# Padded, full-array attention products for the 64 last rows of each sequence, placed behind w_in's, in a two-layer kernel

## The chip, the cores and the metric

The kernel runs on one core of a Trainium2 chip. The metric is the device time of one execution in microseconds, the median of several runs. A profiled execution has a span (first to last instruction) and a time of its own.

## What is computed

Attention with a sliding window of 128 keys and a linear bias per head, then two feed-forward layers over the 2304 rows (4 sequences of 576), all in fp32. Cut to what matters, the reference is:

```python
batch, n_heads, seq, head_dim = (4, 8, 576, 64)
scores = scale * q @ k.T                       # per batch and head
scores = where((rel >= 0) & (rel < 128), scores + slopes[h] * -abs(rel), -1e9)
attn = softmax(scores)                         # over the keys
x = (attn @ v).transpose(0, 2, 1, 3).reshape(B * S, H * D)       # 2304 x 512
h = x @ w_in;  x = relu(h) ** 2 @ w_out        # 512 -> 2048 -> 512
h = x @ w2_in; x = (h * tanh(softplus(h))) @ w2_out
```

## The kernel before

The 2304 rows are cut into five **blocks** (`blocks`, lines 118 to 124): block 0 is rows 0 to 511 of sequence 0, block 1 gathers the **last 64 rows** (512 to 575) of all four sequences, blocks 2 to 4 are rows 0 to 511 of sequences 1 to 3. All five pass through layer 1, then all five through layer 2, in the order 0, 2, 3, 4, 1; so block 1 is stored last.

Attention is cut into **units**: a unit of kind "q" is 256 query rows of one head, a unit of kind "e" the last 64 rows of one sequence for two heads, e = 0 and 1, that lie in the two halves of the partitions. Units 0 to 15 (block 0) run ahead of everything; units 16 to 31 are the 16 "e" units of block 1; units 32 to 79 are "q" units of blocks 2 to 4. The main loop (lines 694 to 740) runs block j through layer 1 in 16 **steps** `fc`, one per 128 columns of w_in, and beside each step of block j goes one unit of block j + 1, in three stages spread over three steps: scores and softmax of unit i + 2, transposition of unit i + 1, value products of unit i. So the "e" units run beside the steps of j = 0. The order on each engine is the order in which the program writes the instructions.

One step of the program, in order: `w_tick1` (j = 0 only: prepares weights on ScalarE, L109 and L85), `u_softmax2` (normalises p of unit i + 1), `front` (loads, and `u_scores` of unit i + 2), `relu2_b` (L577, VectorE: low part g[1] of the previous step), `u_softmax1`, `w_tick2` (VectorE: L91, L94, L97, L114, and the weights' load L80), `m_h` (12 products x by w_in into h: L483 to L485), `relu2_a` (ScalarE: r, then squares gg and g: L566, L569, L572), the first half of `m_out` (g by w_out of the previous step: L511 to L513), a second weights' tick, `turned` (`u_transpose` L376, copy L397, two GpSimd selections L399 that write pT), the second half of `m_out`. The value products `u_av` (L448 for "e" units, L434 for "q" units) stand behind `relu2_a`, but for "e" units from fc = 1 on (`soon`) right behind `front`, ahead of `m_h`.

Products of layer 1 and 2 are done in three parts of a one-pass 32-bit type (hi by hi, lo by hi, hi by lo). The "e" units and block 0's units use plain fp32 products. An "e" unit's scores (L311) are two products of 64 rows by 64 columns of the array, one per head in its own quadrant, 192 columns long; its values (L448) are four products whose results go to 64 of the array's 128 columns: two over 128 keys (urv) and two over 64 (urw), each 64 columns long. A "q" unit's values (L434) likewise go to one column half per head. PSUM tiles of scores, transposed p and values come from a ring of three (`ps_a`); h has one tile. pT of units from 16 on has one buffer.

Loads are all issued by SyncE (SP) in program order. An "e" unit loads q and k (L225, one load), v (L238) and the last 64 keys' v (L239, two buffers). At the end `m_evac` (lines 555 to 558) copies block 1's result (L540 on ScalarE, L541 on VectorE) and stores it with two loads-out of 256 KB from SP, each two sequences.

Of the kernel before, what the change touches and what calls it, by code (L numbers as in the profile page):

```python
# [8 lines left out]
F32 = mybir.dt.float32  # L9
# [5 lines left out]
ALU = mybir.AluOpType  # L15
# [3 lines left out]
P = 128  # L19
B, H, S, D = 4, 8, 576, 64  # L20
# [13 lines left out]
def two_layers(  # L34
# [16 lines left out]
    nc = tc.nc  # L51
# [76 lines left out]
    x32 = {}  # L128
# [78 lines left out]
    def u_load(i):  # L207
        kind, j, off, b, s0, h = units[i]
        u = ustate[i] = Unit()
        if i < NU0:  # L210
            return
        if place[i] not in raws:
            raws.clear()
            raws[place[i]] = ap["raw"].tile([P, 640], F32, tag="uraw", name=f"uraw{i}")
        u.raw = raws[place[i]]
        if kind == "q":
            u.nk = 384 if s0 else 256
            u.nb = u.nk // P
            r = rows(i)
            nc.sync.dma_start(  # L220
                out=u.raw[r, 0 : 256 + u.nk],
                in_=qkT[b, h, r, 2 * s0 : 2 * s0 + 256 + u.nk],
            )
        else:
            nc.sync.dma_start(out=u.raw[:, 0:256], in_=qkE[b, h])  # L225

    def u_vload(i):
        kind, j, off, b, s0, h = units[i]
        if i < NU0:
            return  # L230
        u = ustate[i]
        u.rv = ap["raw"].tile([P, 3, D], F32, tag="urv", name=f"urv{i}", bufs=4)
        if kind == "q":
            k0 = 1 if s0 else 0
            nc.sync.dma_start(out=u.rv[:, 0 : u.nb, :], in_=vP[b, h, :, k0 : k0 + u.nb, :])
        else:
            u.rw = ap["raw"].tile([64, 2, D], F32, tag="urw", name=f"urw{i}")
            nc.sync.dma_start(out=u.rv[:, 0:2, :], in_=vE[b, h])  # L238
            nc.sync.dma_start(out=u.rw, in_=vF[b, h])  # L239

    def u_split(i):
        kind, j, off, b, s0, h = units[i]
# [40 lines left out]
    def u_scores(i):  # L283
        kind, j, off, b, s0, h = units[i]
        u = ustate[i]
        u.ps = ps_a.tile([P, 2, 256], F32, tag="a", name=f"sc{i}")
        if kind == "q":
            for s in range(2):
                k0 = s * P if s0 else 0
                n = 256 if s0 or s else P  # L290
                o = u.ps[:, s, 256 - n :]
                if i < NU0:

                    q, kv = pair[h // 2]
                    c, m = 2 * s0 + h % 2 * 256 + s * P, max(0, s0 + s * P - P)
                    nc.tensor.matmul(o, q[:, c : c + P], kv[:, m : m + n], start=True, stop=True)
                    continue
                if plain_s(i):
                    qk = u.raw[rows(i)]
                    sq, kk = qk[:, s * P : (s + 1) * P], qk[:, 256 + k0 : 256 + k0 + n]  # L300
                    nc.tensor.matmul(o, sq, kk, start=True, stop=True)
                    continue
                sq = u.hi[:, s * P : (s + 1) * P]
                nc.tensor.matmul(o, sq, u.hi[:, 256 + k0 : 256 + k0 + n], start=True, stop=False)  # L304
                nc.tensor.matmul(o, sq, u.lo[:, k0 : k0 + n], start=False, stop=True)  # L305
        else:

            for e in range(2):
                own = slice(e * D, (e + 1) * D)
                o, qk = u.ps[own, 0, 0:192], u.raw[own]  # L310
                nc.tensor.matmul(o, qk[:, 0:D], qk[:, D:256], start=True, stop=True)  # L311

    def probs(i, s):
        kind, j, off, b, s0, h = units[i]
# [63 lines left out]
    def u_unfold(i):  # L378

        kind, j, off, b, s0, h = units[i]  # L380
        u = ustate[i]
        e = 0 if kind == "e" else i % 2
        if e:
            u.pT = ustate[i - 1].pT
        elif i < NU0:
            t = wp.tile([P, 2 * DM], F32, tag=f"wh{8 + i // 2 % 4}", name=f"pT{i}")
            u.pT = t.rearrange("p (e m c) -> p e m c", e=2, m=4)
        else:
            u.pT = ap["w"].tile([P, 2, 4, P], F32, tag="pT", name=f"pT{i}", bufs=1)
        if i < NU0:  # L390
            copy = nc.vector.tensor_copy if i == NU0 - 1 else nc.scalar.copy
            a = 0 if s0 else 1
            copy(u.pT[:, e, a:, :], u.pt[:, a:, :])
            return

        n, m = (2, P) if kind == "q" else (1, D)
        nc.scalar.copy(u.p[:, 0:n], u.pt[:, 0:n])  # L397
        for k, a, r, sign, op in ((0, 0 if s0 else 1, P, 1, ALU.is_gt), (1, 0, m, -1, ALU.is_ge)):
            nc.gpsimd.affine_select(  # L399
                out=u.pT[0:r, e, k : 2 * n : 2, :][:, a:],  # L400
                in_=u.p[0:r, a:n],
                pattern=[[0, n - a], [0, P // m], [-sign, m]],
                compare_op=op,
                fill=0.0,
                base=0,
                channel_multiplier=sign,
            )

    def u_av(i):
# [32 lines left out]
            ustate.pop(i - 1)  # L442
        else:
            o = ps_a.tile([P, 512], F32, tag="a", name=f"o{i}")
            for blk, (r, v) in enumerate(((P, u.rv), (64, u.rw))):
                for e in range(2):
                    c = slice(e * D, (e + 1) * D)
                    nc.tensor.matmul(  # L448
                        o[c, 0:D], v[:, e, :], u.pT[0:r, 0, blk, c], start=blk == 0, stop=blk == 1
                    )  # L450
            nc.scalar.copy(x32[j][h][:, off : off + D], o[:, 0:D])
        ustate.pop(i)


# [67 lines left out]
    def m_evac(l, j, parts=(0, 1)):  # L522
# [11 lines left out]
        for p in parts:  # L534
# [13 lines left out]
            if len(runs) == 1:  # L548
# [2 lines left out]
                dst = out[row : row + 2 * P, :].rearrange("(e p) d -> p e d", e=2)  # L551
                nc.sync.dma_start(out=dst, in_=ev)
                continue
            ends = out.rearrange("(b s) d -> b s d", b=B)
            for e in range(2):
                b = 2 * (2 * p + e)
                s0, m = runs[b][1:]
                nc.sync.dma_start(out=ends[b : b + 2, s0 : s0 + m, :], in_=ev[:, e, :])

    def relu2_a(j, fc):  # L560
        n = size[j]
# [24 lines left out]
    ap["raw"] = actx.enter_context(tc.tile_pool(name="araw", bufs=2))  # L586
    ap["spl"] = actx.enter_context(tc.tile_pool(name="aspl", bufs=2))
    ap["w"] = actx.enter_context(tc.tile_pool(name="aw", bufs=2))
    bias_sb = ap["w"].tile([P, 1 + H, 256], BF16, name="bias_sb", bufs=1)
    biasA_sb = wp.tile([P, 2 * DM], F32, tag="wh7", name="biasA_sb")  # L590
    biasA_sb = biasA_sb.bitcast(BF16).rearrange("p (h c) -> p h c", h=H)
# [29 lines left out]
    def turned(i):  # L621
        u_transpose(i)
        u_unfold(i)
# [70 lines left out]
    for j in range(NB - 1):  # L694
        for fc in range(FC):
            step = j * FC + fc
            last = fc == FC - 1
            av, tr, sc = ([i] if i < NU else [] for i in range(NU0 + step, NU0 + step + 3))
            soon = units[av[0]][0] == "e" and fc > 0
            if j == 0:  # L700
                w_tick1(0)
            for i in tr:
                u_softmax2(i)
            for i in sc:
                front(i)
            for i in av if soon else []:
                u_av(i)
            if pend is not None:
                relu2_b(pend)
            for i in sc:  # L710
# [5 lines left out]
                for c in range(2):  # L716
                    x_split(j + 1, c, xp)
            pend = relu2_a(j, fc)
            for i in av if not soon else []:
                u_av(i)  # L720
            if last:
                for c in range(2, KC):
                    x_split(j + 1, c, xp)
            if prev is not None:
                m_out(*prev, 0)
            if j == 0 and turn["at"] < NW + 4:
                w_tick(0)
            for i in tr:
                turned(i)
            if prev is not None:  # L730
                m_out(*prev, 1)
# [181 lines left out]
```

## Time and profile before

| | |
|---|---|
| runs | 943.62, 945.62, 945.96 us; median 945.62 |
| profiled execution: its time, its span | 945.08 us, 943.3 us |
| busy: TensorE, VectorE, ScalarE, GpSimd | 96%, 43%, 44%, 21% |
| w_in products of block 0 (16 steps), first and last start | 41.83 and 157.85 us |

The page shows for each engine the time in which it executed something, and the list of waits what ended the idle stretches. Products overlap: the start of one to the start of the next is what a product costs, not its duration. An order of instructions in time is read per engine; a number in brackets is the idle time just before the instruction, with the instruction that ended it. The view by stretches gives the length, then each engine's busy time and count (PE, PEld for weight loads, DVE, ACT, POOL), the clock granted to TensorE, the DMA engines' busy share and GB/s. PE is TensorE, DVE VectorE, ACT ScalarE, POOL GpSimd, SPq SyncE's queue.

### The profile page before, as it was taken

How to read it: one execution, taken by the hardware profiler on the slowest of the kernel's cores; microseconds unless marked ns; L12 is line 12 of the kernel's file. 1: busy time of each engine (PE TensorE's matmuls, PEld its weight loads, DVE VectorE, ACT ScalarE, POOL GpSimd, SP SyncE). 2: the span in 40 equal slices, each digit the busy share in tenths (PEclk: the TensorE clock that was granted, in tenths of full speed). 3: DMA queues.
4: the chain of work that ended last, by engine and by line, in shares of the span. 5: the costliest groups of instructions: out<-in, count | busy, mean ns of one | idle time of the engine just before them, and what ended most of it. 6: DMA issues, size and time to landing. Idle time of an engine off the chain costs nothing.

```text
span 943.3 us, 13014 instructions
## 1 busy us (share of the span) xinstructions
PE 909.6 (96%) x4680; PEld 743.1 (79%) x4680; DVE 409.1 (43%) x1043; ACT 419.5 (44%) x1017; POOL 200.1 (21%) x314
## 2 busy tenths in 40 slices
PE   7989999999999999999999999999999999999993
PEld 5666667999778877887788888888888888888893
DVE  6887887665433353333699662111212111111110
ACT  6866665666554455444577633222212222222220
POOL 4311114676555555552000000000000000000000
PEclk9999999999999999999999999999999999999997
DMA  8365551433222222230664430020002000200100
GB/s 238 125 201 167 166 173 60 138 87 91 80 61 53 62 92 65 78 102 1 202 199 157 134 112 1 1 89 1 1 1 90 1 0 1 67 1 1 45 1 23
DMA packets 40293, 74.71 MB, mean 79 GB/s; under 512 B 4388, under 2 KB 18340, under 8 KB 40228
## 3 DMA queue, kind: packets, MB, share of 16 engines
q1 hardware_dynamic: 40228, 73.88, 24.9%
q8 instruction: 37, 0.61, 0.3%
q14 instruction: 28, 0.23, 0.1%
HBM read 64.42 MB, written 9.44 MB: 78 GB/s over the span
## 4 chain that ended last, share of the span: by engine, by line
PE 87%; ACT 6%; DVE 2%; POOL 2%; issue 1%; SPq 1%; DMA 1%; POOLq 0%; DVEq 0%
PE h L483 14%; PE h L484 14%; PE h L485 14%; PE o L516 7%; PE o L517 7%; PE o L518 7%; PE o L511 6%; PE o L512 6%; PE o L513 6%; PE o L434 3%; POOL pT L399 1%; PE sc L305 1%; PE sc L304 1%; PE pt L376 1%; ACT gg L569 1%; ACT r L566 1%
## 5 line engine op out<-in xcount | busy, mean ns | idle before, releaser
L483 PE MATMUL h<-xh,wh 128*128 128x512 f32 (+1 forms) x640 | 238.5, 373 | 1.5 <-ACT r L566 1.5
L484 PE MATMUL h<-xl,wh 128*128 128x512 f32 (+1 forms) x640 | 236.4, 369 | 0.0
L485 PE MATMUL h<-xh,wl 128*128 128x512 f32 (+1 forms) x640 | 236.0, 369 | 0.0
L760 ACT ACTIVATE t<-h 128x512 f32<-128x512 f32 (+1 forms) x80 | 44.4, 555 | 290.3 <-PE h L485 215.9
L766 DVE TENSOR_TENSOR g<-t,g 128x512 fp32r<-128x512 f32 (+1 forms) x80 | 50.9, 636 | 203.8 <-ACT g L761 203.8
L483 PEld LDWEIGHTS h<-xh,wh 128*128 128x128 f32 x640 | 120.8, 189 | 22.7 <-ACT r L566 2.0
L485 PEld LDWEIGHTS h<-xh,wl 128*128 128x128 f32 x640 | 121.0, 189 | 20.7
L484 PEld LDWEIGHTS h<-xl,wh 128*128 128x128 f32 x640 | 121.1, 189 | 19.2
L511 PE MATMUL o<-g,wh 128*128 128x512 f32 (+1 forms) x320 | 126.0, 394 | 0.0
L512 PE MATMUL o<-g,wh 128*128 128x512 f32 (+1 forms) x320 | 118.5, 370 | 1.2 <-DVE g L577 1.2
L513 PE MATMUL o<-g,wl 128*128 128x512 f32 (+1 forms) x320 | 118.4, 370 | 0.0
L516 PE MATMUL o<-wh,g 128*128 128x512 f32 x288 | 112.2, 390 | 0.0
L517 PE MATMUL o<-wl,g 128*128 128x512 f32 x288 | 112.2, 390 | 0.0
L518 PE MATMUL o<-wh,g 128*128 128x512 f32 x288 | 112.0, 389 | 0.0
L339 ACT ACTIVATE p<-p,st 128x128 f32<-128x128 f32 (+1 forms) x144 | 59.5, 415 | 85.8 <-DVE st L328 85.7
L399 POOL TENSOR_SCALAR_AFFINE_SELECT pT<-p 128x256 f32<-128x256 f32 (+2 forms) x128 | 59.0, 480 | 131.1 <-ACT p L397 130.5
L577 DVE TENSOR_TENSOR g<-gg,g 128x512 fp32r<-128x512 f32 (+1 forms) x80 | 57.6, 720 | 55.8 <-POOL gg L571 53.6
L566 ACT ACTIVATE r<-h 128x512 f32<-128x512 f32 (+1 forms) x80 | 44.0, 549 | 84.4 <-PE h L485 84.4
L511 PEld LDWEIGHTS o<-g,wh 128*128 128x128 f32 x320 | 60.1, 188 | 13.4 <-issue 2.2
L512 PEld LDWEIGHTS o<-g,wh 128*128 128x128 f32 x320 | 60.4, 189 | 10.3 <-DVE g L577 2.3
L513 PEld LDWEIGHTS o<-g,wl 128*128 128x128 f32 x320 | 60.2, 188 | 10.5
L518 PEld LDWEIGHTS o<-wh,g 128*128 128x128 f32 x288 | 54.1, 188 | 11.5
(69 smaller groups left out, 1172.4 us busy)
## 6 DMA issues: line engine op xcount, KB each, us to landing
wraw<-in_w SPq DMA_DIRECT2D x64, 512.0 KB, 4.3
uraw<-in_qkT SPq DMA_DIRECT2D x24, 320.0 KB, 3.0
uraw<-in_qkT SPq DMA_DIRECT2D x24, 256.0 KB, 2.7
x<-x1d SPq DMA_DIRECT2D x16, 256.0 KB, 4.3
out_x<-ev SPq DMA_DIRECT2D x8, 512.0 KB, 2.9
x1d<-ev SPq DMA_DIRECT2D x10, 256.0 KB, 2.3
urv<-in_vP SPq DMA_DIRECT2D x24, 96.0 KB, 2.6
uraw<-in_qkE SPq DMA_DIRECT2D x16, 128.0 KB, 2.0
```

What stands on the lines that cost most here:

```text
L339: nc.scalar.activation(probs(i, s), probs(i, s), AF.Exp, bias=u.st[:, s : s + 1], scale=-1.0, accum_out=u.st[:, 2 + s : 3 + s],)
L399: nc.gpsimd.affine_select(out=u.pT[0:r, e, k : 2 * n : 2, :][:, a:], in_=u.p[0:r, a:n], pattern=[[0, n - a], [0, P // m], [-sign, m]], com ...
L483: nc.tensor.matmul(ph[:, 0:n], wh[:, cs], xh[:, 0:n], start=c == 0, stop=False)
L484: nc.tensor.matmul(ph[:, 0:n], wh[:, cs], xl[:, 0:n], start=False, stop=False)
L485: nc.tensor.matmul(ph[:, 0:n], wl[:, cs], xh[:, 0:n], start=False, stop=c == KC - 1)
L511: nc.tensor.matmul(o[:, r], wh[:, ws], g[:, 0, r], start=first, stop=False)
L512: nc.tensor.matmul(o[:, r], wh[:, ws], g[:, 1, r], start=False, stop=False)
L513: nc.tensor.matmul(o[:, r], wl[:, ws], g[:, 0, r], start=False, stop=last)
L516: nc.tensor.matmul(o, g[:, 0, es], wh[:, ws], start=first, stop=False)
L517: nc.tensor.matmul(o, g[:, 0, es], wl[:, ws], start=False, stop=False)
L518: nc.tensor.matmul(o, g[:, 1, es], wh[:, ws], start=False, stop=last)
L577: nc.vector.tensor_tensor(g[:, 1, 0:n], gg[:, 0:n], g[:, 0, 0:n].bitcast(F32), op=ALU.subtract)
```

## The change

The "e" units' products use the whole array. q of the two heads is loaded into the two diagonal quarters of a 128 x 128 tile `qd` (two buffers, zero elsewhere, set once by GpSimd), so one product of 192 columns gives both heads' scores. v of the last 64 keys is loaded into the upper half of `vd` (three buffers, lower half zero), and two products of 128 columns give the values of both heads, each with the other head's probabilities as well; two copies of 64 x 64 on ScalarE take the two diagonal quarters. The second GpSimd selection covers 128 rows instead of 64. `soon` is gone: the values of all units stand behind `relu2_a`. For j > 0 `turned` stands right behind the values, ahead of the first half of `m_out`. pT has two buffers. Block 1's last store is four stores of 128 KB, one per sequence, in turn from SP and ScalarE's queue.

```diff
@@ u_load
-            nc.sync.dma_start(out=u.raw[:, 0:256], in_=qkE[b, h])
+            u.qd = qd[i % len(qd)]
+            for e in range(2):
+                c = slice(e * D, (e + 1) * D)
+                nc.sync.dma_start(out=u.qd[c, c], in_=qkE[b, h, c, 0:D])
+            nc.sync.dma_start(out=u.raw[:, 0:192], in_=qkE[b, h, :, D:256])
@@ u_vload
-            u.rw = ap["raw"].tile([64, 2, D], F32, tag="urw", name=f"urw{i}")
+            u.rw = vd[i % len(vd)]
             nc.sync.dma_start(out=u.rv[:, 0:2, :], in_=vE[b, h])
-            nc.sync.dma_start(out=u.rw, in_=vF[b, h])
+            nc.sync.dma_start(out=u.rw[0:64], in_=vF[b, h])
@@ u_scores
-            for e in range(2):
-                own = slice(e * D, (e + 1) * D)
-                o, qk = u.ps[own, 0, 0:192], u.raw[own]
-                nc.tensor.matmul(o, qk[:, 0:D], qk[:, D:256], start=True, stop=True)
+            nc.tensor.matmul(
+                u.ps[:, 0, 0:192], u.qd, u.raw[:, 0:192], start=True, stop=True
+            )
@@ u_unfold
-            u.pT = ap["w"].tile([P, 2, 4, P], F32, tag="pT", name=f"pT{i}", bufs=1)
+            u.pT = ap["w"].tile([P, 2, 4, P], F32, tag="pT", name=f"pT{i}", bufs=2)
...
-        for k, a, r, sign, op in ((0, 0 if s0 else 1, P, 1, ALU.is_gt), (1, 0, m, -1, ALU.is_ge)):
+        for k, a, sign, op in ((0, 0 if s0 else 1, 1, ALU.is_gt), (1, 0, -1, ALU.is_ge)):
             nc.gpsimd.affine_select(
-                out=u.pT[0:r, e, k : 2 * n : 2, :][:, a:],
-                in_=u.p[0:r, a:n],
+                out=u.pT[:, e, k : 2 * n : 2, :][:, a:],
+                in_=u.p[:, a:n],
@@ u_av
-            for blk, (r, v) in enumerate(((P, u.rv), (64, u.rw))):
-                for e in range(2):
-                    c = slice(e * D, (e + 1) * D)
-                    nc.tensor.matmul(
-                        o[c, 0:D], v[:, e, :], u.pT[0:r, 0, blk, c], start=blk == 0, stop=blk == 1
-                    )
-            nc.scalar.copy(x32[j][h][:, off : off + D], o[:, 0:D])
+            for blk, v in enumerate((u.rv[:, 0:2, :], u.rw)):
+                v = v.rearrange("p e d -> p (e d)")
+                nc.tensor.matmul(
+                    o[:, 0:P], v, u.pT[:, 0, blk, :], start=blk == 0, stop=blk == 1
+                )
+            for e in range(2):
+                c = slice(e * D, (e + 1) * D)
+                nc.scalar.copy(x32[j][h][c, off : off + D], o[c, c])
@@ m_evac
-            ends = out.rearrange("(b s) d -> b s d", b=B)
-            for e in range(2):
-                b = 2 * (2 * p + e)
-                s0, m = runs[b][1:]
-                nc.sync.dma_start(out=ends[b : b + 2, s0 : s0 + m, :], in_=ev[:, e, :])
+            for k, (b, s0, m) in enumerate(runs):
+                row = b * S + s0
+                src = ev[k % 2 * m : (k % 2 + 1) * m, k // 2, :]
+                (nc.sync, nc.scalar)[k % 2].dma_start(out=out[row : row + m, :], in_=src)
@@ two_layers, ahead of the loads
+    qd = [ap["raw"].tile([P, P], F32, name=f"qd{n}", bufs=1) for n in range(2)]
+    vd = [ap["raw"].tile([P, 2, D], F32, name=f"vd{n}", bufs=1) for n in range(3)]
+    for t in qd + vd:
+        nc.gpsimd.memset(t, 0.0)
@@ main loop
-            soon = units[av[0]][0] == "e" and fc > 0
...
-            for i in av if soon else []:
-                u_av(i)
...
             pend = relu2_a(j, fc)
-            for i in av if not soon else []:
+            for i in av:
                 u_av(i)
+            for i in tr if j > 0 else []:
+                turned(i)
...
-            for i in tr:
+            for i in tr if j == 0 else []:
                 turned(i)
             if prev is not None:
                 m_out(*prev, 1)
```

Where this moves TensorE's instructions is seen in two places. The first is the step fc = 6 of j = 0, from the end of the step before (names: sc scores, o with pT values, h the w_in products, o_0 the w_out products, pt the transposition). Before:

```order
L513 MATMUL o_0_3_727<-g_0_4_965,wl_4_837 128x512
L311 MATMUL sc_1087<-uraw_928 64x192 x2
L448 MATMUL o_1096<-pT_1069,urv_930 64x64 x2
L448 MATMUL o_1096<-pT_1069,urw_931 64x64 x2
L483 MATMUL h_0_6_1114<-xh_309,wh_6_998 128x512
...
L485 MATMUL h_0_6_1114<-xh_588,wl_6_999 128x512
L511 MATMUL o_0_0_724<-g_0_5_1046,wh_5_917 128x512
```

With the change:

```order
L519 MATMUL o_0_3_739<-g_0_4_969,wl_4_848 128x512
L312 MATMUL sc_1095<-uraw_937,qd_99 128x192
L489 MATMUL h_0_6_1116<-xh_323,wh_6_1007 128x512
...
L491 MATMUL h_0_6_1116<-xh_602,wl_6_1008 128x512
L452 MATMUL o_1135<-pT_1077,urv_941 128x128
L452 MATMUL o_1135<-pT_1077,vd_102 128x128
L517 MATMUL o_0_0_736<-g_0_5_1049,wh_5_927 128x512
```

The values have moved from ahead of the twelve w_in products to behind them, and both groups have half as many, wider products.

The second place is a step of block 2 with values. Before, TensorE's order behind its w_in products is:

```order
L485 MATMUL h_2_5_3343<-xh_2953,wl_5_918 128x512
L434 MATMUL o_3362<-pT_3246,urv_3138 64x256
...
L434 MATMUL o_3362<-pT_3246,urv_3200 64x128
L511 MATMUL o_2_0_3100<-g_2_4_3294,wh_4_836 128x512
...
L513 MATMUL o_2_1_3101<-g_2_4_3294,wl_4_837 128x512
L376 MATMUL pt_3374<-ident,p_3274 128x128 x2
L511 MATMUL o_2_2_3102<-g_2_4_3294,wh_4_836 128x512
```

With the change:

```order
L491 MATMUL h_2_5_3337<-xh_2954,wl_5_928 128x512
L438 MATMUL o_3356<-pT_3234,urv_3132 64x256
...
L438 MATMUL o_3356<-pT_3234,urv_3194 64x128
L379 MATMUL pt_3362<-ident,p_3268 128x128 x2
L517 MATMUL o_2_0_3101<-g_2_4_3288,wh_4_847 128x512
...
L519 MATMUL o_2_1_3102<-g_2_4_3288,wl_4_848 128x512
L517 MATMUL o_2_2_3103<-g_2_4_3288,wh_4_847 128x512
```

The transpositions now follow the values directly, and the twelve w_out products are no longer parted.

## Rows read from the trace of the kernel before

**Rows 1.** The page: busy time of the engines; TensorE's granted clock by slices.

```profile
PE 909.6 (96%) x4680; PEld 743.1 (79%) x4680; DVE 409.1 (43%) x1043; ACT 419.5 (44%) x1017; POOL 200.1 (21%) x314
...
PEclk9999999999999999999999999999999999999997
```

**Rows 2.** List of waits: engine, line, releaser, us in total, times, longest.

```profile
PE o L448 <- POOL pT L399: 9.8, 27, 2.7
```

**Rows 3.** TensorE in order of time: start us, us, line, [idle before].

```profile
80.90 0.50 PE L483 MATMUL h<-xh,wh 128*128 128x512 f32 x1
...
86.73 0.54 PE L311 MATMUL sc<-uraw 64*64 64x192 f32 x4
87.46 0.34 PE L448 MATMUL o<-pT,urv 128*64 128x64 f32 x4 [0.19 <-POOL pT L399]
88.15 0.33 PE L448 MATMUL o<-pT,urw 64*64 64x64 f32 x4 [0.35 <-POOL pT L399]
88.42 0.50 PE L483 MATMUL h<-xh,wh 128*128 128x512 f32 x1
```

**Rows 4.** ScalarE in order of time, the same step.

```profile
83.98 0.60 ACT L566 ACTIVATE r<-h 128x512 f32<-128x512 f32 x1 [2.35 <-PE h L485]
...
86.74 0.24 ACT L397 COPY p<-pt 128x128 f32<-128x128 f32 x1
...
88.53 0.21 ACT L451 COPY x<-o 128x64 f32<-128x64 f32 x1 [0.15 <-PE o L448]
```

**Rows 5.** GpSimd in order of time, the same step.

```profile
87.12 0.98 POOL L399 TENSOR_SCALAR_AFFINE_SELECT pT<-p 128x128 f32<-128x128 f32 x2 [6.53 <-ACT p L397]
```

**Rows 6.** VectorE in order of time, the same step.

```profile
84.54 0.69 DVE L97 SCALAR_TENSOR_TENSOR wf<-wraw,wf 128x512 int32<-128x512 int32 x1
86.30 0.69 DVE L114 TENSOR_TENSOR wl<-wf,wh 128x512 fp32r<-128x512 f32 x1 [1.07 <-ACT wh L109]
```

**Rows 7.** TensorE in order of time, units of block 0.

```profile
31.61 0.60 PE L373 MATMUL pt<-ident,p 128*128 128x128 f32 x4
32.05 1.03 PE L296 MATMUL sc<-kv,qq 128*128 128x256 f32 x4
32.91 0.49 PE L373 MATMUL pt<-ident,p 128*128 128x128 f32 x3
```

**Rows 8.** TensorE in order of time, two steps of block 2.

```profile
273.90 0.39 PE L513 MATMUL o<-g,wl 128*128 128x512 f32 x1
...
274.58 0.40 PE L512 MATMUL o<-g,wh 128*128 128x512 f32 x1
...
278.72 0.39 PE L485 MATMUL h<-xh,wl 128*128 128x512 f32 x1
...
280.39 0.39 PE L512 MATMUL o<-g,wh 128*128 128x512 f32 x1
```

**Rows 9.** Busy time in one stretch; PEclk is the granted clock.

```profile
50.00:60.00 10.00, 9.46 (x44) 6.99 (x43) 7.62 (x19) 6.45 (x17) 0.98 (x2) 0.86 0.54 179
```

**Rows 10.** VectorE in order of time, steps 0 and 1 of block 0.

```profile
45.52 0.69 DVE L114 TENSOR_TENSOR wl<-wf,wh 128x512 fp32r<-128x512 f32 x1
...
51.86 0.69 DVE L114 TENSOR_TENSOR wl<-wf,wh 128x512 fp32r<-128x512 f32 x1
```

**Rows 11.** TensorE in order of time, w_in's first product of fc = 2.

```profile
58.42 0.50 PE L483 MATMUL h<-xh,wh 128*128 128x512 f32 x1
```

**Rows 12.** VectorE, ScalarE, TensorE in order of time, end of block 0.

```profile
142.15 1.11 DVE L97 SCALAR_TENSOR_TENSOR wf<-wraw,wf 128x512 int32<-128x512 int32 x1
...
151.47 0.60 ACT L566 ACTIVATE r<-h 128x512 f32<-128x512 f32 x1 [1.92 <-PE h L485]
...
164.61 0.50 PE L512 MATMUL o<-g,wh 128*128 128x512 f32 x1 [1.24 <-DVE g L577]
```

**Rows 13.** The page's DMA issues: count, KB each, us to landing.

```profile
x1d<-ev SPq DMA_DIRECT2D x10, 256.0 KB, 2.3
```

**Rows 14.** SP in order of time: the last two stores before.

```profile
929.12 1.33 SPq L558 DMA_DIRECT2D out_x<-ev  x2
```

## The prediction

> **What bounds the kernel now.** I read the page first. TensorE is busy in 96% of the span and its clock stands at the upper level nearly throughout [rows 1], so there is little idle time to win, and the list of waits says where some of it is: the value products of the last rows (L448) stood still for 9.8 us in 27 places until GpSimd had written pT [rows 2]. They all lie in the first block, j = 0. There I took TensorE's own instructions in order of time for one step [rows 3]. From the first w_in product at 80.90 to the scores at 86.73 stand 24 products and one transposition, 5.83 us without a hole. From 86.73 to the next w_in product at 88.42 stand only the scores (L311) and values (L448) of one small unit, yet they take 1.69 us, 0.54 of it idle before L448. One step is 7.52 us.
>
> Why L448 waits is read backwards through the other engines. ScalarE starts r when w_in's products end (83.98), then squares twice, converts weights (L109, L85) and only then copies the turned p (L397, 86.74) [rows 4]; GpSimd's two selections follow, 87.12 to 88.10 [rows 5]; and L448 stands in TensorE's queue ahead of the next w_in products. So w_in -> r -> ... -> pT -> L448 -> w_in is a ring, and the step is as long as the ring. ScalarE itself was idle for 2.35 us before r, and VectorE waits 1.07 us per step at L114 for L109 [rows 4, 6]. Its own work is thus 7.52 - 1.07 = 6.45 us a step: no engine is full. From block 2 on, TensorE has no such hole.
>
> **The change, part by part.**
> *Values behind w_in, steps fc = 1 to 15.* The ring is cut: pT is needed one w_in group later, about 3 us. What bounds the step next is TensorE's own work or VectorE's 6.45 us.
>
> *Full-array products.* The trace has no such product of a last-rows unit; the nearest is the plain fp32 score of block 0: two products of 256 columns take 32.05 to 32.91, 0.86 us for 512 columns [rows 7]. So the new scores (192 columns) cost 0.32 us and the two value products (256 columns together) 0.43. What the old ones took is 1.69 less the 0.54 idle: 1.15. Entering and leaving fp32 within the full array shows no price of its own: four transpositions among other fp32 products take 31.61 to 32.05, 0.11 us each [rows 7], and two set between w_out's products stretch L513 at 273.90 to L512 at 274.58, two products of 0.24 (5.83 less 0.11, by 24), to 0.68, so they cost 0.20, about 0.1 each again [rows 8]. I allow nothing for it. New step: 5.83 + 0.32 + 0.43 = 6.58 us; the gain is 0.94. VectorE's 6.45 is the floor, and 6.95 (below) the other end.
>
> The Trainium skill speaks against this part: its page "TensorEngine Tiling (Array Packing)", Theoretical Speedup, says that with a dimension of 64 or less the array works as independent tiles, up to twice as fast, and two products of 64 columns on separate column halves would indeed stream half as long as the padded pair does. By that rule alone the values become dearer by 0.21 us per unit and only the wait is won; the sum would be 937 (rival F). Its Key Properties say on the other side that changing the tiling mode drains TensorE. The rows decide: after the wait had ended, L448's second pair took 0.27 us (88.15 to 88.42) for 64 columns, which are 0.11 us at the rate above [rows 3, 7].
>
> *The first steps.* At fc = 1, L448 waited 2.7 us, its longest wait [rows 2], and in the 10 us behind it the trace shows a granted clock of 0.86 of full speed, so some 2.8 us of them ran at 1.2 GHz, which cost about 1.4 us [rows 9]. Now w_in of fc = 1 starts when its weights are there (L114 ends at 46.21), and one new step later, near 53.0, w_in of fc = 2, which in turn needs the L114 that ends at 52.55 [rows 10]. Before, it began at 58.42 [rows 11]: gain 5.4 us. The two loops behind are then close together: TensorE at 53.0, VectorE at 52.55.
>
> *Twelve steps, fc = 2 to 14:* 12 x 0.94 = 11.3 us.
>
> *What is given back at the end of block 0.* The values' copies are two of about 0.2 us instead of one (L451: 0.21), and they now stand between g and L109 in ScalarE's queue [rows 4]. Through steps 2 to 13 that queue has room. In step 14 it has none: from r at 151.47 the chain r, g, L109, L114, softmax, exp, r, L577 ends in w_out's L512 at 164.61, where TensorE already waits 1.24 us [rows 12]. That chain is 13.1 us long and is not shortened; the copies lengthen it twice by 0.4: 0.8 us. And near 142 VectorE's operations stretch (L97 takes 1.11 us instead of 0.69 [rows 6, 12]) while GpSimd splits the next block's q and k. In the old order the idle 1.07 swallowed that, now it does not: about 1.1 us. Net for block 0: 5.4 + 11.3 - 1.9 = 14.8 us.
>
> *More loads, selections over 128 rows, zeroing, a second pT.* SP issues two more small loads a step and no longer waits at vF's load for the old values (three vd instead of two urw), so the weights behind them start no later. Selection k = 1 covers 128 rows; selections of both heights are in the 0.98 us [rows 5], and GpSimd has over 6 us of rest behind them. The five memsets come at the start, where GpSimd has nothing to do. All nothing.
>
> *Transpositions beside the values, 48 units of blocks 2 to 4.* In every second step they now directly follow the column-tiled products L434. Around these, L485 at 278.72 to L512 at 280.39 are 1.67 us for 0.48 of ordinary products and 512 columns (0.86): 0.33 goes into getting in and out [rows 8]. If the transpositions share the way out, 0.1 x 24 = 2.4 us are won; if each pair pays half of the 0.33 itself, 48 x 0.17 = 8 us are lost. p is ready a step earlier, so no wait comes. I take the row on the transpositions, which showed only their columns, at the old and at the new place, plus a little sharing: 0.3 us won.
>
> *Last store.* After the last copy two issues of 128 KB from two queues replace one of 256 KB, which lands in some 2.3 us elsewhere [rows 13]. Between 0.6 lost (a second queue must be emptied) and 0.6 won (one of SP's two issues, 1.33 together [rows 14]) I take 0.2, as less data lies behind the last issue. The Trainium skill, Key Constraints of "Trainium Kernel Development and Optimization", says that queues share the 16 DMA engines and that a second issuing engine saves only issue time; it would bound this gain by the same 0.6.
>
> **Sum.** 14.8 + 0.3 + 0.2 = 15.3 us. The profiled execution took 945.08 (0.54 under the median of the runs, 945.62): 929.8, so I say 930.
>
> **Rivals.**
> *B. VectorE becomes the bound.* Where GpSimd ran beside it, its operations grew by up to 1.6 times [rows 12]. If the selections, now spread over w ticks, stretch two of them, the step is 6.45 + 0.5 = 6.95: 12 x 0.37 = 4.5 lost, and 1 more at the end: 935. Against it: L577 beside the selections kept its length. Late weights would look alike.
> *C. The transpositions pay for the change of mode:* 8 us lost as above, 938.
> *F. The padded products only cost.* If the old pairs overlapped and their 0.27 us was latency that more work behind it would have hidden, a step wins the 0.54 of waiting less 0.21 (half of the new 0.43): 0.33 instead of 0.94, over 12 steps 7.3 us less: 937. It is the Trainium skill's rule for small tiles, above. Against it: the w_in product did follow at 88.42, only when the 0.27 were over.
> *D. Slower: the clock.* Values and transpositions together make, every second step, a stretch of over 1.2 us of narrow products. If the clock fell there as after the wait of 2.7 us, at 1.4 us a fall, 24 falls cost 34 us: 930 + 34 = 964; from 11 falls on the kernel is slower than before. Against D: the clock's line shows 9 also in the first slices, where units consist of just such products [rows 1].
> *E. Nothing comes of it.* The chain at the end of block 0 would have to swallow all but a little, 943 to 946; but it starts only at r of fc = 14, whose start TensorE set [rows 12], so I see no way.
>
> **Chances.** Forecast 0.65; B 0.14; C 0.09; F 0.03; D 0.04; E 0.05. About 0.3% (2.8 us) can be told from no change. Forecast, B, C and F are faster by more: 0.91; E is the same but for a little: 0.05; D slower: 0.04. The forecast's own range is 925.5 (VectorE's floor, 1.6 more; 2 from sharing; 0.4 at the store) to 933. To hold 8 in 10 the range goes on over B and F to C's 938; D and E stay outside.
>
> **What would show it.** Right: in block 0 no wait of value products for GpSimd, steps of 6.45 to 6.7 us, w_in of fc = 2 near 53 and of fc = 14 near 132, full clock from 45 us on, a wait at w_out's second product near 150, of 1 us or more. Wrong: VectorE without a pause and steps near 7 (B); the stretch from L485 to the second w_out product longer than 1.67 + 0.20 (C); granted clock under 1 after 170 us (D). The forecast falls if the steps of block 0 stay above 7.2.

## The result, and the profile after

The changed kernel takes **921.36 us** (median of four runs, 917.53 to 921.48) against 945.79: ratio 0.974, 95% interval 0.9726 to 0.9753. It is faster by 24.4 us where 15.6 were predicted, and the time lies below the range. Three of the four runs lie at 921.3 to 921.5 with a mean granted clock of 0.995; the one at 917.53 has 0.999.

The page of the changed kernel answers to [rows 1]:

```profile
PE 902.6 (98%) x4584; PEld 748.1 (81%) x4584; DVE 411.0 (45%) x1043; ACT 422.7 (46%) x1033; POOL 207.6 (23%) x319
...
PEclk9999999999999999999999999999999999999999
```

TensorE is 2 points busier, with 96 instructions fewer by the page's count. Its list of waits has lost the line of [rows 2]. Of the lines below, the first two stood in the list before as well (kv 2.3 us; r 1.5 us, in the second step of the last block that layer 1 takes, block 4). w_out's second product (L518, before L512) waits in two places, where it waited once, for 1.24 us [rows 12]; the wait of L379 is new:

```profile
PE sc L300 <- DMA kv<-in_kvA: 2.7, 1, 2.7
PE h L489 <- ACT r L571: 1.7, 2, 1.5
PE o L518 <- DVE g L582: 1.3, 2, 0.7
PE pt L379 <- DVE p L358: 1.1, 2, 0.6
```

A step of block 0, TensorE in order of time (start, length, line), answers to [rows 3]:

```profile
82.13 0.38 PE L452 MATMUL o<-pT,urv 128*128 128x128 f32 x2
82.35 0.39 PE L452 MATMUL o<-pT,vd 128*128 128x128 f32 x2
82.49 0.48 PE L517 MATMUL o<-g,wh 128*128 128x512 f32 x1
...
85.45 0.49 PE L312 MATMUL sc<-uraw,qd 128*128 128x192 f32 x2
85.64 0.53 PE L489 MATMUL h<-xh,wh 128*128 128x512 f32 x1
...
88.55 0.38 PE L452 MATMUL o<-pT,urv 128*128 128x128 f32 x2
```

From values to values it is 6.42 us without a wait (6.41 on average): values 0.36, scores 0.19, the rest the 24 products and the transposition. VectorE, next to it, has one pause of 0.17 us a step and repeats after 6.34 (82.65 to 88.99): the two are now nearly level.

```profile
82.65 0.29 DVE L331 CUSTOM_DVE_ANT_0 p<-sc,biasE_sb 128x128 f32<-128x128 f32 x1 [0.17 <-DVE sc L285]
...
84.05 0.69 DVE L97 SCALAR_TENSOR_TENSOR wf<-wraw,wf 128x512 int32<-128x512 int32 x1
84.66 0.69 DVE L114 TENSOR_TENSOR wl<-wf,wh 128x512 fp32r<-128x512 f32 x1
...
88.99 0.29 DVE L331 CUSTOM_DVE_ANT_0 p<-sc,biasE_sb 128x128 f32<-128x128 f32 x1 [0.17 <-DVE sc L285]
```

The end of block 0 on TensorE answers to [rows 12]: four waits, 2.2 us together, and behind the last one products that follow each other after 0.43 us instead of 0.23 until 152.8. The granted clock from 149.65 to 152.80 is 0.50, the level of 1.2 GHz.

```profile
141.84 0.50 PE L518 MATMUL o<-g,wh 128*128 128x512 f32 x1 [0.58 <-DVE g L582]
...
146.45 0.38 PE L489 MATMUL h<-xh,wh 128*128 128x256 f32 x1 [0.40 <-ACT xh L468]
...
148.34 0.41 PE L379 MATMUL pt<-ident,p 128*128 128x128 f32 x2 [0.57 <-DVE p L358]
...
149.65 0.79 PE L518 MATMUL o<-g,wh 128*128 128x512 f32 x1 [0.68 <-DVE g L582]
150.25 0.63 PE L519 MATMUL o<-g,wl 128*128 128x512 f32 x1
150.67 0.63 PE L517 MATMUL o<-g,wh 128*128 128x512 f32 x1
```

The surprise is behind the last instruction. In the kernel before, SP's last issues end at 930.45 [rows 14] and the span ends at 943.3. The view by stretches shows what ran there: nothing but DMA, at a share of 0.12 to 0.13, as much as two busy engines of sixteen (last two columns: DMA share, GB/s).

```profile
930.00:935.00 5.00, 0.00 (x0) 0.00 (x0) 0.00 (x0) 0.00 (x0) 0.00 (x0) 0.85 0.12 34
935.00:940.00 5.00, 0.00 (x0) 0.00 (x0) 0.00 (x0) 0.00 (x0) 0.00 (x0) 0.50 0.13 52
940.00:945.00 5.00, 0.00 (x0) 0.00 (x0) 0.00 (x0) 0.00 (x0) 0.00 (x0) 0.50 0.05 19
```

With the change the last copy ends at 915.70 and the span at 919.5; the share is 0.35 over a stretch that is partly empty:

```profile
915.00:920.00 5.00, 0.00 (x0) 0.00 (x0) 0.69 (x1) 0.00 (x0) 0.00 (x0) 0.74 0.35 105
```

So the **tail**, the time from the end of the last copy to the end of the span, shrank from 13.4 us (943.3 - 929.88) to 3.8. The last copies, before and after:

```profile
929.19 0.69 DVE L541 COPY ev<-o 128x512 f32<-128x512 f32 x1 [2.99 <-PE o L518]
```

```profile
915.01 0.69 DVE L547 COPY ev<-o 128x512 f32<-128x512 f32 x1 [2.99 <-PE o L524]
```

### The profile page after: what moved, and what is told of

It reads as the page before. It is cut to its first block, busy times and chain, and to the rows that moved or that the text cites. A ratio compares the mean times of both kernels' runs of the same rounds, so it can differ in the third digit from the quotient of the medians.

```text
span 919.5 us, 12922 instructions
## 1 busy us (share of the span) xinstructions
PE 902.6 (98%) x4584; PEld 748.1 (81%) x4584; DVE 411.0 (45%) x1043; ACT 422.7 (46%) x1033; POOL 207.6 (23%) x319
## 4 chain that ended last, share of the span: by engine, by line
PE 90%; DVE 4%; ACT 2%; DMA 1%; SPq 1%; issue 1%; POOL 0%; DVEq 0%; POOLq 0%; ACTq 0%
PE h L489 13%; PE h L491 13%; PE h L490 13%; PE o L522 7%; PE o L523 7%; PE o L524 7%; PE o L518 7%; PE o L517 7%; PE o L519 6%; PE o L438 3%; PE pt L379 1%; PE sc L308 1%; PE sc L309 1%; DMA kv<-in_kvA 1%; PE sc L300 1%
## 5 line engine op out<-in xcount | busy, mean ns | idle before, releaser
L491 PE MATMUL h<-xh,wl 128*128 128x512 f32 (+1 forms) x640 | 236.1, 369 | 0.4 <-DVE wl L114 0.3
L491 PEld LDWEIGHTS h<-xh,wl 128*128 128x128 f32 x640 | 120.7, 189 | 21.6 <-DVE wl L114 1.3
L518 PE MATMUL o<-g,wh 128*128 128x512 f32 (+1 forms) x320 | 119.2, 372 | 1.3 <-DVE g L582 1.3
L403 POOL TENSOR_SCALAR_AFFINE_SELECT pT<-p 128x256 f32<-128x256 f32 (+1 forms) x128 | 67.7, 547 | 86.4 <-ACT p L401 84.8
L582 DVE TENSOR_TENSOR g<-gg,g 128x512 fp32r<-128x512 f32 (+1 forms) x80 | 57.9, 723 | 55.5 <-POOL gg L576 33.9
L518 PEld LDWEIGHTS o<-g,wh 128*128 128x128 f32 x320 | 60.9, 190 | 10.6 <-DVE g L582 2.0
L576 POOL TENSOR_TENSOR gg<-r 128x512 f32<-128x512 f32 (+1 forms) x48 | 43.6, 908 | 102.6 <-issue 68.9
```

The costliest lines, as they stand in the source:

```text
L403: nc.gpsimd.affine_select(out=u.pT[:, e, k : 2 * n : 2, :][:, a:], in_=u.p[:, a:n], pattern=[[0, n - a], [0, P // m], [-sign, m]], compare ...
L491: nc.tensor.matmul(ph[:, 0:n], wl[:, cs], xh[:, 0:n], start=False, stop=c == KC - 1)
L518: nc.tensor.matmul(o[:, r], wh[:, ws], g[:, 1, r], start=False, stop=False)
L582: nc.vector.tensor_tensor(g[:, 1, 0:n], gg[:, 0:n], g[:, 0, 0:n].bitcast(F32), op=ALU.subtract)
```

## The experiments

All times are medians of four runs beside the kernel before on the same chip. A tail is counted as above.

**1. The new last store alone**, put into the kernel before (its four lines in place of the two-sequence store).

> The kernel before with the new last store alone (four stores of 64 rows, in turn from SP and ScalarE's queue). Theory K: the old store's destination had two sequences as its slowest dimension, so only 2 of the 16 DMA engines carried its 512 KB, and the span ended some 13 us after the last issue; 64 rows outermost spread it over all. Then the time falls by about 9.5 us (the old tail of 13.4 us behind the last copy less the new one's 3.8), to 936 +- 1, and the DMA share behind the last copy rises from 0.12 to over 0.3. Theory P (the prediction's: the old store lands in 2.3 us too, the rest of the gain lies elsewhere): 945 to 946.

Measured: 935.09, ratio 0.9893 (0.9872 to 0.9913), 10.9 us won; the tail is 3.8 us and the DMA share from 930 to 935 us is 0.36. This is what theory K expects, and not theory P.

**2. The changed kernel with the old store.**

```diff
-            for k, (b, s0, m) in enumerate(runs):
...
+            for e in range(2):
+                b = 2 * (2 * p + e)
+                nc.sync.dma_start(out=ends[b : b + 2, s0 : s0 + m, :], in_=ev[:, e, :])
```

> The changed kernel with the old last store (two stores of two sequences each, from SP). Theory K: 921.4 + 9.5 = 931, so that the rest of the change is worth 945.8 - 931 = 15, which is what the prediction had for it (15.1). Theory P: 921.5 to 922.

Measured: 927.14, ratio 0.9809 (0.9793 to 0.9825); the tail is 13.5 us. The tail is again as theory K has it, but the whole is 4 us less than expected. Up to the last copy this profiled execution is 18.7 us ahead of the kernel before, the changed kernel's 14.2, although the two programs are the same up to there. It has the full clock in two places where the changed kernel's has 0.85 (20 to 30 us) and 0.86 (150 to 160 us), and it waits 1.23 us in place of 2.74 in the prologue. 927.14 - 9.7 is 917.4, near the fastest run of the changed kernel (917.53), the one with the clock of 0.999.

**3. All four stores from SP.**

```diff
-                (nc.sync, nc.scalar)[k % 2].dma_start(out=out[row : row + m, :], in_=src)
+                nc.sync.dma_start(out=out[row : row + m, :], in_=src)
```

> The changed kernel with its four last stores all from SP. Theory K: the second queue saves no more than issue time, two issues of 0.6 us behind the last copy, so 921.4 to 922.7. If the second queue was what won the 9.6 us (rival Q: two queues move data side by side, one does not): 929 to 931.

Measured: 920.56, ratio 0.9731 (0.971 to 0.9753); the tail is 4.4 us, 0.6 longer, about one issue (the four take 2.44 us). The second queue is not what won.

**4 and 5. Stores cut into 62 + 2 and into 60 + 4 rows**, eight issues in both.

```diff
+                for a, z in ((0, m - 2), (m - 2, m)):    # 5: m - 4
+                    (nc.sync, nc.scalar)[k % 2].dma_start(
+                        out=out[row + a : row + z, :], in_=src[a:z])
```

> The changed kernel with each last store cut into 62 rows and 2 rows, from the same queue. Theory K with the count of engines as the largest number up to 16 that divides the rows: 62 and 2 both give two engines, so nearly all of the 512 KB goes over two engines again and the time rises by 8 to 11 us, to 930 to 932, with a DMA share of 0.12 behind the last copy. Rival R (what counts is that a store holds one sequence, or less data per store): two issues more per queue, 1.3 us, so 921.4 to 923.

> The changed kernel with each last store cut into 60 rows and 4 rows, from the same queue: as many issues as with 62 and 2. If the count of engines is the largest number up to 16 that divides the rows, 60 rows go over 15 engines and 4 over 4, and the tail behind the last copy, 13.3 us with 62 and 2, is again 4 to 5.5 us (921 to 923). If only powers of two count, 60 rows go over 4 engines, 120 KB each at the 19 GB/s that an engine moved there: a tail of some 7 us and a time of 924 to 925. If the two issues more were what cost, it is as with 62 and 2: 930.

Measured: 931.01 with 62 + 2 (ratio 0.9841, 0.9815 to 0.9867), tail 13.3; 920.5 with 60 + 4 (0.9738, 0.9719 to 0.9757), tail 3.8. Two rows more or less per store are worth 9.5 us of tail. With 62 rows the stretches show the share of two engines again, with 60 rows they do not:

```profile
915.00:920.00 5.00, 0.00 (x0) 0.00 (x0) 0.18 (x1) 0.00 (x0) 0.00 (x0) 0.71 0.12 34
920.00:925.00 5.00, 0.00 (x0) 0.00 (x0) 0.00 (x0) 0.00 (x0) 0.00 (x0) 0.50 0.13 51
925.00:930.00 5.00, 0.00 (x0) 0.00 (x0) 0.00 (x0) 0.00 (x0) 0.00 (x0) 0.50 0.05 20
```

```profile
915.00:920.00 5.00, 0.61 (x3) 0.19 (x1) 0.69 (x1) 0.56 (x1) 0.00 (x0) 0.88 0.34 105
```

So what counts is neither the sequence, the queue nor the size of a store, but the number of its outermost rows. The Trainium skill, page "DMA: Bandwidth & Descriptors", section "Why a DMA increments its semaphore by 16 and not by 1", states it: a DMA goes over the largest number of engines, up to 16, that divides the slowest dimension of both its sides. For two sequences or 62 rows that is 2, for 64 rows 16, for 60 it is 15. The tails agree: 13.5, 13.3, 3.8, 3.8 us (they do not tell 15 engines from 16, but a rule of powers of two, which would give some 7 us with 60 rows, is out). With the two old stores, or with the four of 62 rows from two queues, the share stayed at two in sixteen: the stores did not spread over more engines side by side. Which two engines they were the view does not show.

**6. The values behind w_in alone**: the kernel before without `soon`, with three buffers for urw; quadrant products stay.

```diff
-            for i in av if soon else []:
-                u_av(i)
...
-            for i in av if not soon else []:
+            for i in av:
```

> The kernel before with the values of the last rows behind w_in's products alone (and three buffers for the 64-key v, which that order needs); quadrant products, old store, old place of the transpositions stay. Theory W (the prediction's: a unit's quadrant products cost 1.15 us of TensorE's time): steps of 5.83 + 1.15 = 6.98 us in block 0 where the changed kernel has 6.34 and the kernel before 7.50; the time about 945.8 - 12 x 0.52 - 5 + 2 = 936 to 937. Rival F (their pairs overlap, the 0.27 us behind the second pair was latency that work behind it hides): steps of 6.3 to 6.45, the time 930 to 932, as the changed kernel with the old store.

Measured: 934.07, ratio 0.9887 (0.9872 to 0.9901). w_in's first products follow each other after 7.03 us (88.29 to 95.32), where theory W has 6.98 and rival F 6.45 at most; the time is 2 to 3 us better than W's, for which no run here gives the reason. One step, TensorE in order of time:

```profile
91.23 0.34 PE L448 MATMUL o<-pT,urv 128*64 128x64 f32 x4
91.50 0.33 PE L448 MATMUL o<-pT,urw 64*64 64x64 f32 x4
91.76 0.50 PE L511 MATMUL o<-g,wh 128*128 128x512 f32 x1
...
94.84 0.54 PE L311 MATMUL sc<-uraw 64*64 64x192 f32 x4
95.32 0.50 PE L483 MATMUL h<-xh,wh 128*128 128x512 f32 x1
```

With plenty of ready work behind it each pair of L448 still takes 0.26 to 0.27 us and the scores 0.48: the narrow products' price is real, not a wait that other work would hide. Rival F is out. The Trainium skill's page "TensorEngine Tiling (Array Packing)" has, under Key Properties, that a change of tiling mode drains TensorE; 0.26 us for a pair of 64 columns is in keeping with that, but no run shows that it is the drain that costs. The speedup that its Theoretical Speedup gives small tiles is not seen in groups as short as these: 0.53 us for the four narrow products, 0.36 for the two padded ones.

**7. The full-array products alone**: the changed kernel with the values ahead of w_in's products again.

```diff
                 front(i)
+            for i in av if soon else []:
+                u_av(i)
```

> The changed kernel with the values of the last rows ahead of w_in's products, as before (full-array products, new store kept). Ring theory: the step is again the ring through ScalarE and GpSimd; the full-array products take 0.1 to 0.3 us out of its 7.50 (one product less to start, none of the way out of the quadrants), so 7.2 to 7.4 us a step and 13 x (7.3 - 6.34) = 12.5 us more than the changed kernel, plus the wait of some 2 us at fc = 1: 933 to 937. Rival (the full-array form alone cuts the step): 6.4 to 6.7 us a step, 921 to 926.

Measured: 932.77, ratio 0.9869 (0.9853 to 0.9885), steps of 7.41 us (85.71 to 93.12, by L312). The ring of waits is back in the list:

```profile
PE o L452 <- POOL pT L403: 9.4, 26, 3.4
```

Steps of block 0 are thus 7.50 us with neither part, 7.03 with the order, 7.41 with the form, 6.41 with both. While the ring bounds the step, shorter products mostly lengthen the wait. In whole times the order alone won 11.0 us (945.11 to 934.07), the form alone 12.3, of which the new store has 9.6, and everything but the store 18.8 (number 2). The second pT buffer was not tried by itself.

**8. The transpositions of blocks 2 to 4 at their old place.**

```diff
-            for i in tr if j > 0 else []:
-                turned(i)
...
-            for i in tr if j == 0 else []:
+            for i in tr:
```

> The changed kernel with the transpositions of blocks 2 to 4 between w_out's halves again. The prediction had 0.3 us for this term, between 2.4 won and 8 lost. By the changed kernel's own steps, whose lead grows by about 0.07 us in two steps of blocks 2 and 3, the new place is worth 24 x 0.07 = 1.7 us less what it loses at the changes of block (0.6 at two of them): the time 921 to 923.5, and the lead over the kernel before flat through blocks 2 and 3. By rival C (each transposition pair pays for the change of mode at the new place) it would be 913 to 918.

Measured: 921.7, ratio 0.9752 (0.9734 to 0.977), which the runs do not tell from the changed kernel's 921.36. The profiled executions do, by the starts of r (layer 1 takes the blocks in the order 0 to 4). From block 1's second step to the last step of block 3 the changed kernel gains 0.8 us on this one: some 0.07 in two steps, a loss of 0.65 where block 2 begins, of which 0.26 comes back two steps later, and 0.1 to 0.2 won where block 3 begins. Another 0.4 is won between the first two steps of block 1. There the old place has one long wait, where the changed kernel has two shorter ones, at L379 and at L518, of 1.25 us together:

```profile
149.09 0.65 PE L518 MATMUL o<-g,wh 128*128 128x512 f32 x1 [1.64 <-DVE g L582]
```

So the new place is worth 0.8 to 1.2 us in these two executions. Rival C is out.

**9 and 10. The end of each block reordered.** Number 9 changes the place of the low part of g, of the exponentials and of a block's first transposition; number 10 only the first, in the two places marked:

```diff
+            if last and pend is not None:      # low part of g
+                relu2_b(pend)
+                pend = None
             for i in tr:
                 u_softmax2(i)
...
-            for i in sc:
+            for i in sc if not last else []:
                 u_softmax1(i)
...
-            for i in tr if j > 0 else []:
+            for i in tr if j > 0 and fc > 0 else []:
...
             if last:
+                for i in sc:
+                    u_softmax1(i)
+                relu2_b(pend)      # low part of g
+                pend = None
```

> The changed kernel with the end of each block reordered: in the last step VectorE takes the low part of g (the one w_out waits for) ahead of the unit's normalisation, the exponentials of the next unit come behind r and the squares, the low part of the last g is written at once; the first transposition of a block stands between w_out's halves again. Theory: the 2.8 us that the end of block 0 gives back are this chain on ScalarE and VectorE, with TensorE idle for 2.2 us between 140 and 150 us and, behind that, at half its clock for some 3 us; without the chain 2 to 3.5 us come back, and 0.4 at each of two later ends: 917 to 919.5, with TensorE busy for 9 of the 10 us from 140 to 150 and a full clock behind. Rival: the wait is at the weights or GpSimd's splits, which this leaves: 921.

> Of the reordering at the end of the blocks only the low part of g (ahead of the normalisation in the last step, and at once for the last g); the exponentials and the first transposition stay where the changed kernel has them. If VectorE's late low part is what TensorE waits for (its waits before w_out's second product, 0.58 and 0.68 us), some half comes back: r of the second step of block 1 lies 1 to 1.5 us earlier from block 0's first r than in the changed kernel, and with the fall of the clock gone 2.5 to 3.5. If the exponentials ahead of r on ScalarE are the chain, under 0.5.

Measured: number 9 takes **914.48** (ratio 0.9687, 0.9666 to 0.9709), number 10 takes 918.7 (0.9714, 0.9697 to 0.9732). Number 9 is below its forecast of 917 to 919.5. It is the best version of the study, 0.7% ahead of the changed kernel, with an interval that does not touch its. From block 0's first r to r of block 1's second step it is 5.2 us shorter than the changed kernel, number 10 3.0, as forecast for the low part with the clock up. What answers in number 9 (stretches: length, PE, PEld, DVE, ACT, POOL, clock, DMA share, GB/s):

```profile
140.00:150.00 10.00, 9.91 (x55) 8.19 (x54) 8.41 (x25) 7.46 (x23) 5.37 (x8) 1.00 0.23 71
150.00:160.00 10.00, 10.00 (x80) 9.20 (x79) 6.74 (x23) 7.04 (x25) 6.57 (x12) 1.00 0.55 182
```

and in the changed kernel:

```profile
140.00:150.00 10.00, 7.70 (x41) 5.90 (x40) 6.70 (x16) 5.14 (x15) 3.84 (x6) 0.97 0.14 38
150.00:160.00 10.00, 10.00 (x64) 8.71 (x64) 6.23 (x20) 5.96 (x19) 3.92 (x8) 0.86 0.56 181
```

The idle 2.2 us are gone and the clock stays up. The low part alone gives 3.0 of the 5.2 us; the other 2.2 belong to the exponentials and the first transposition together, which no run separates.

**11. Number 9 with the second weights' load behind the last pair's q and k.**

```diff
-    w_tick(0)
-    for p in (2, 3):
-        p_load(p)
-        pv_load(p)
+    p_load(2)
+    pv_load(2)
+    p_load(3)
+    w_tick(0)
+    pv_load(3)
...
-        if n in (4, 6, 9, 13):
+        if n in (4, 12, 14, 16):
```

> The reordered kernel with the second weights' load of 512 KB behind q and k of the last pair of heads, and its conversion later. The prologue's longest wait of TensorE (1.2 to 3.2 us near 20 us, for kv of the last pair) lies where the DMA engines are full (share 1.0 from 12 to 22 us). Theory: the pair arrives 1.5 us earlier, the wait shrinks below 1.5 us, and the clock, which fell behind every wait of 2.6 us or more so far, stays up: 0.5 to 3 us less than the reordered kernel's 914.5. Rival: the weights' pipeline then holds up the first steps: 915 to 918.

Measured: 916.61, ratio 0.9702 (0.9687 to 0.9716): no gain. The wait near 20 us shrank to 0.74, with a full clock in 20 to 30, but TensorE is busy for only 7.29 us between 30 and 40, with a wait of 1.81 for GpSimd's p, and the clock falls (0.86, then 0.80 in 40 to 50). The time is the rival's. Its reason fits, but is not shown: from 31.38 to 34.05 VectorE converts the moved weights, ahead of the softmax that this p comes from.

## Why the prediction was wrong, step by step

| term, us won | predicted | measured |
|---|---|---|
| before block 0 | 0 | -0.65 |
| first steps | 5.4 | 5.5 |
| 12 steps | 11.3 | 12.8 |
| end of block 0 | -1.9 | -4.2 |
| transpositions | 0.3 | 0.8 |
| last store | 0.2 | 9.6 |
| sum | 15.3 | 23.8 |

The measured column is taken from the two profiled executions, which differ by 945.08 - 921.42 = 23.7: starts of w_in's first products (41.83 and 42.48; fc = 2 at 58.42 and 53.57; fc = 14 at 148.42 and 130.79), of r in block 1's second step and in layer 1's last step of block 3 (lines below, before and after), and the tails.

```profile
171.63 0.36 ACT L566 ACTIVATE r<-h 128x256 f32<-128x256 f32 x1
...
440.33 0.60 ACT L566 ACTIVATE r<-h 128x512 f32<-128x512 f32 x1 [0.82 <-PE h L485]
```

```profile
158.21 0.36 ACT L571 ACTIVATE r<-h 128x256 f32<-128x256 f32 x1
...
426.14 0.60 ACT L571 ACTIVATE r<-h 128x512 f32<-128x512 f32 x1 [0.81 <-PE h L491]
```

*The step that failed is the last store*, put at 0.2 us and worth 9.6. "Replace one of 256 KB, which lands in some 2.3 us elsewhere": the landing time was borrowed from stores of another shape [rows 13], because the page gave none for this one, and the bounds of 0.6 either way were bounds on issues only. The trace held the answer: 12.9 us between the last issue's end and the span's, with the share of two engines at work. I read the waits of the engines and never the stretch behind the last instruction. The sentence from the Trainium skill, Key Constraints of "Trainium Kernel Development and Optimization", that a second queue saves only issue time, is right (0.6 us in number 3) and was beside the point. The whole distance between forecast and result is here: without the tail's 9.4 us too little, the sum is off by 0.9. That the rest comes so close is partly luck: in number 2, with the full clock up to the last copy, the same program is 18.7 us ahead there, where 15.1 were predicted. The steps won more than the sum had, and in the changed kernel's profiled execution the prologue and the end of block 0 lost it again.

*The ring, the first steps:* right in mechanism and sum. No value product waits for GpSimd in block 0, and 5.5 us were won for 5.4. But w_in of fc = 2 follows fc = 1 after 7.34 us, not after one new step: L491 waits 0.34 for the low weights of L114, and fc = 1 in turn started 0.6 sooner after fc = 0 than the prediction had it.

*The step:* 6.41 instead of 6.58. The full-array products cost 0.36 and 0.19 us, not 0.43 and 0.32: by the rate of block 0's scores [rows 7] they were a third too dear. The old products' 1.15 us were right to 0.05 (number 6: 7.03 for 6.98). VectorE's floor was 6.34, not 6.45: the bracket of 1.07 at L114 [rows 6] is less than the wait cost, because without a wait L114 starts 0.08 before L97's record ends (84.66; 84.05 + 0.69). TensorE stays the bound by 0.07. Rival B did not come.

*The end of block 0:* the chain and its place were right, and in number 2, at full clock, the size too: the same stretch gives back 1.8 us where 1.9 were predicted (2.2 if it is counted to three steps later). How these parts share it, 0.8 for copies and 1.1 for stretched operations, no run shows. In the profiled execution of the changed kernel it gives back 4.2: the clock stood at 0.50 for 3.15 us behind the waits, which is 1.6 us by itself; the rest of the difference was not taken apart. D had such a price, but sought the fall beside the values, where the clock never left 1.00. The sign "a wait at w_out's second product near 150, of 1 us or more" came as 0.68; with the transpositions at their old place it is 1.64 (number 8).

*The transpositions:* 0.8 us by the table and 0.8 to 1.2 by number 8, with 0.3 predicted, inside the bounds. "p is ready a step earlier, so no wait comes" did not hold in the first step of blocks 1 and 2, where L379 waits for p (0.57 and 0.53). In block 1 that wait only stands in place of a longer one; in block 2 0.4 us are lost.

## What to carry to other kernels

Measure the time between the last instruction and the end of the span, and the DMA share in it, before anything else: a store whose outermost dimension was 2 ran here at the share of two engines, and a missing landing time is itself a sign. Cutting a ring of waits and shortening what stands in it were worth 0.47 and 0.09 us a step one by one and 1.09 together, so price a change by the bound that is left after both. When a wait on one engine is removed, follow the next block's first step: the operations that were late without harm (here the low part of g behind a normalisation) become the wait.

## What was not expected of the hardware

*As few as two DMA engines*, by the share of 0.12 to 0.13, carried 512 KB in some 13 us, and a cut of 64 rows into 62 + 2 is enough to fall back to that, while 60 + 4 is not (numbers 2, 4, 5).

*The clock differs between executions of one program.* The first r of block 0 starts between 43.0 us (number 2) and 47.95 (number 9) although the two kernels have the same program up to there; the clock granted in 20 to 30 us is 1.00 and 0.66. Before the fall in number 9 TensorE stood waiting for the last pair's kv:

```profile
21.01 1.62 PE L300 MATMUL sc<-kv,qq 128*128 128x128 f32 x4 [3.16 <-DMA kv<-in_kvA]
```

Waits of 2.25 us in the kernel before and of 2.50 in number 6 were followed by no fall, one of 1.81 in number 3 by one to 0.87 in that stretch; the rows give no rule, and the 2.6 us in number 11's expectation is none. The starts of block 0 thus differ by nearly 5 us in a program of 920; the runs of the changed kernel spread over 4.

*VectorE's operations stretch while GpSimd works.* L358 takes 0.42 us where GpSimd is idle and 1.27 beside its splits, L582 0.67 and up to 1.49. VectorE, then GpSimd, in the changed kernel:

```profile
139.37 1.27 DVE L358 TENSOR_TENSOR p<-p,st 128x256 f32<-128x256 f32 x1
140.57 1.22 DVE L582 TENSOR_TENSOR g<-gg,g 128x512 fp32r<-128x512 f32 x1
...
148.11 1.49 DVE L582 TENSOR_TENSOR g<-gg,g 128x512 fp32r<-128x512 f32 x1
...
245.74 0.42 DVE L358 TENSOR_TENSOR p<-p,st 128x256 f32<-128x256 f32 x1
```

```profile
139.34 1.02 POOL L253 TENSOR_TENSOR ulo<-uraw,uhi 128x384 fp32r<-128x384 f32 x1
140.44 0.80 POOL L255 TENSOR_TENSOR uhi<-uraw,uhi 64x256 fp32r<-64x256 f32 x1
...
147.89 1.16 POOL L253 TENSOR_TENSOR ulo<-uraw,uhi 128x384 fp32r<-128x384 f32 x1
```
